# Block-product groups: one bank with four products, copied out on the way, in place of four banks with sums

## The chip, the cores and the metric

One core of a Trainium2 chip runs the whole program. The metric is the device time of one execution in microseconds. The core's engines work from queues of their own and meet at semaphores: TensorE (PE in the profile; PEld is its weight load), VectorE (DVE), ScalarE (ACT), GpSimd (POOL) and SyncE (SP), which issues most DMAs. TensorE writes into eight PSUM banks; each bank holds a tile of 128 x 448 fp32 here.

## The reference

The program computes an attention with mixed heads, then two gated or squared feed-forward layers, in fp32 accuracy:

```python
def _moe_ref(x, w1, w2, w3, w_out):
    a = x @ w1
    b = x @ w2
    h = a * b @ w3
    return (h @ w_out).astype(np.float32)

def _moe2_ref(x, w_in, w_out):
    h = np.maximum(x @ w_in, 0.0)
    return (h * h @ w_out).astype(np.float32)
```

x has 1792 tokens of 768 features (attention output); w1 and w2 go to 1024, w3 and w_out of the first layer are multiplied together ahead of use (their product is 1024 x 768), w_in goes to 2048 and the last w_out back to 768.

## The kernel before, in words

Each fp32 operand is split into a high part and a low part, and each product of a 128 x 128 weight block with 128 x 448 values takes three matmuls (high x high, high x low, low x high: `mm3`, L60). The tokens are done in two halves of 896, each in two tiles t = 0, 1 of 448.

Attention comes first. After it, `Moe.run` works through a list of units. A unit is a `l1` product (x by w1 or w2), `p34` (w3 by w_out), `ly` (a*b by that product, giving y), a "quad" or `l4_part` (h by the last w_out, in four groups of rows `gr`). The quads are what the change touches. A quad is a 2 x 2 block product (two 128-row output blocks r = 0, 1, two token tiles t = 0, 1) done with seven block products in place of eight. Its left factors are the weight blocks A(r, c) and four sums S1 to S4 of them, its right factors are B11, B21, B22 and four differences T1 to T4. With ks = 3 each product is 9 matmuls, so a quad is 63. There are 24 quads: 8 for x by w1 and w2 in the second half (`l1_quad`, j = 0 to 3, named q00, q01, q10, ... for w1 and w2 in turn) and 8 for y by w_in in each half (`l3_quad`, named qh00 to qh07 and qh10 to qh17). The hidden-layer quads come in runs between groups of `l4_part`: 0, 1, 2; 3, 4; 5, 6, 7 in the first half, and 0, 1, 2; 3, 4; 5, 6; 7 in the second. The last quad of each run (`hold`) lets its later work wait some steps longer.

A quad's result is finished by the other engines. In `quad.run`, the seven products t = 0 to 6 (this t is a step) go to four banks: A, B, C, A, B, C, D. ScalarE copies s1 (product 0) and s5 (product 2) out, VectorE forms u2 (product 1 plus s1) and u3 (bank B after its second product, plus s1), and `done(r, t, x, y)` takes each of the four results, as a bank alone (0, 0) or as a sum of two operands. `done` of a hidden-layer quad then applies relu and square, and `split_late` makes the high part on ScalarE (L723) and the low part on VectorE (L724). For (1, 1) the sum is on GpSimd, and relu and square on ScalarE (L877, L878); elsewhere they are one VectorE instruction (L881).

The order on every queue is the order in which the code issues, and nothing reorders it. `stage(s, run)` issues one step: loads, the sums S of weight blocks on VectorE (`combine`, L144) for products that are four or five steps ahead, the high part of a weight three steps ahead on ScalarE (`high`, L120), the low part two steps ahead on GpSimd (`rest`, L148), then whatever was put into `self.late[0]` for this step, then the matmuls of the product with the work that follows from it. `self.late[n]` holds work to be issued n steps after the next one's start.

Of the kernel before, what the change touches and what calls it, by code (L numbers as in the profile page):

```python
# [37 lines left out]
def fused_kernel(ctx, tc, q, k, v, w_pre, w_post, w1, w2, w3t, wo, win, wo2, eye, out):  # L38
# [494 lines left out]
    class Moe:  # L533
# [52 lines left out]
        def stage(self, s, run=None):  # L586
            w = self.w
            ok = lambda i: 0 <= i < len(self.pieces)
            quad = lambda i: self.pieces[i][1] if ok(i) and self.pieces[i][0] is None else None
            if ok(s + 6) and not quad(s + 6):  # L590
                w.load(s + 6, *self.pieces[s + 6][:2])
            if quad(s + 7) and self.pieces[s + 7][2] == ("A", 0, 0):
                w.load_quad(quad(s + 7))
            if quad(s + 5) and self.pieces[s + 5][2] == ("S", 2, 0):
                w.combine(quad(s + 5), 1)
                w.combine(quad(s + 5), 2)
            if quad(s + 4) and self.pieces[s + 4][2] in (("S", 3, 0), ("S", 4, 0)):
                w.combine(quad(s + 4), self.pieces[s + 4][2][1])
            if quad(s + 3):
                _, q, name = self.pieces[s + 3]  # L600
                w.ft[s + 3] = q.f[name]
                w.place(s + 3)
                w.high(s + 3)
            if ok(s + 4):
                w.narrow(s + 4)
            if ok(s + 3) and not quad(s + 3):
                for part in range(2):
                    w.join(s + 3, part)
                to = self.pieces[s + 3][2:]
                w.place(s + 3, self.wot[to[0]] if to and to[0] else None)  # L610
                if not self.pieces[s + 3][1]:
                    w.high(s + 3)
            if ok(s + 2):
                w.rest(s + 2, nc.vector if self.pieces[s + 2][2:] and not quad(s + 2) else nc.gpsimd)
            if run:
                self.late.append([])
                for f in self.late.pop(0):
                    f()
                run()
            if ok(s + 3) and not quad(s + 3) and self.pieces[s + 3][1]:  # L620
                w.high(s + 3)
                if s + 3 in self.keep:
                    w.save(s + 3, self.keep[s + 3])
# [172 lines left out]
        def quad(self, name, src, x, ks, done):  # L796
            q = type("Quad", (), {})()
            q.name, q.f, q.src = name, {}, src
            A, S_ = (lambda r, c: ("A", r, c)), (lambda n: ("S", n, 0))
            plan = [  # L800
                (A(0, 0), "B11", "A"), (S_(2), "T2", "B"), (S_(1), "T1", "C"), (A(0, 1), "B21", "A"),
                (S_(3), "T3", "B"), (S_(4), "B22", "C"), (A(1, 1), "T4", "D"),
            ]
            bank, tmp = {}, {}

            def us(n):
                tmp[n] = self.tile(f"{n}{name}")
                return tmp[n]

            def run(ws, t):  # L810
                _, xn, bk = plan[t]
                start = bk not in bank
                if start:
                    bank[bk] = self.psum(f"q{name}{bk}")
                acc = bank[bk]
                mm3(acc, [(self.chunk([ws[t]], c), x()[xn, c]) for c in range(ks)], start, True, not start)
                if t == 0:
                    nc.scalar.activation(us("s1"), acc, AF.Copy)
                elif t == 1:
                    self.add(us("u2"), acc, tmp["s1"])  # L820
                elif t == 2:
                    nc.scalar.activation(us("s5"), acc, AF.Copy)
                elif t == 3:
                    done(0, 0, acc)
                elif t == 4:
                    self.add(us("u3"), acc, tmp["s1"])
                    done(1, 1, tmp["u3"], tmp["s5"])
                elif t == 5:
                    done(0, 1, acc, tmp["u2"])
                else:  # L830
                    done(1, 0, acc, tmp["u3"])

            return [(None, q, n) for n, _, _ in plan], run

        def l1_quad(self, j, second):
            end = j == 3

            def done(r, t, x, y=None):
                m = 2 * j + r
                eng = nc.gpsimd if r and t and not end else nc.vector  # L840
                if not second:
                    a = self.xy["a", m, t] = self.tile(f"a1_{m}_{t}")
                    if y is None:
                        nc.scalar.activation(a, x, AF.Copy)
                    else:
                        self.add(a, x, y, eng)
                    return
                ab = self.xy["ab", 1, m, t] = self.pair(f"ab1_{m}_{t}")
                p = self.tile(f"p1_{m}_{t}")
                mul = lambda: nc.vector.tensor_tensor(p, x if y is None else p, self.xy["a", m, t], ALU.mult)  # L850
                if eng is nc.gpsimd:
                    self.late[0].append(lambda: self.add(p, x, y, eng))
                    self.late[1].append(mul)
                    self.split_late(ab, p, 2, 3)
                    return
                if y is not None:
                    self.add(p, x, y)
                mul()
                self.split_late(ab, p, 0, 0 if end else 1)

            src = [w12d[int(second), 2 * j + r] for r in range(2)]
            return self.quad(f"{j}{int(second)}", src, lambda: self.xq, 3, done)
# [1 line left out]
        def l3_quad(self, hf, j):  # L864
# [3 lines left out]
            def done(r, t, x, y=None):  # L868
# [3 lines left out]
                if y is None:  # L872
                    nc.scalar.activation(p, x, AF.Relu)
                    square = lambda: nc.scalar.activation(p, p, AF.Square)
                elif r and t and not end:
                    def square():
                        nc.scalar.activation(p, p, AF.Relu)  # L877
                        nc.scalar.activation(p, p, AF.Square)  # L878
                    self.late[0].append(lambda: self.add(p, x, y, nc.gpsimd))
                else:  # L880
                    square = lambda: nc.vector.scalar_tensor_tensor(p, p, 0.0, p, ALU.max, ALU.mult)  # L881
                    self.add(p, x, y)
                if end and y is not None:
                    square()
                    self.split_late(hb, p, 0, 0)
                    return
                at = {(0, 0): 0, (1, 1): 1, (0, 1): 0, (1, 0): 0}[r, t]
                if hold:
                    at = {(0, 0): 3, (1, 1): 2, (0, 1): 2, (1, 0): 1}[r, t]
                self.late[at].append(square)  # L890
                self.split_late(hb, p, at + 1, at + 2)

# [3 lines left out]
        def yquad(self, hf, n, t, acc):  # L896
# [28 lines left out]
            if name == "B22":  # L925
# [3 lines left out]
                hi("B22", acc)  # L929
                lo("T2", r("T2"))  # L930
                lo("B22", acc)
                diff("T4", r("B21"), r("T2"))
                hi("T3", r("T3"))
                hi("T4", r("T4"))
                lo("T3", r("T3"), G if j < 2 else V)
                lo("T4", r("T4"), G if j < 2 else V)
                return
            nc.scalar.activation(raw(name), acc, AF.Copy)
            if name != "B12":
# [50 lines left out]
        def l4_part(self, hf, gr, es):  # L990
            def run(ws, s):
# [2 lines left out]
                if hf == 0 and gr > 1:  # L994
                    self.quad_x(6 * gr - 12 + es[0])
                accs = {(e, t): self.psum(f"l4{hf}_{gr}_{e}_{t}") for e in es for t in range(2)}
                for cs, order in (((0, 1), (0, 1)), ((2,), (0, 1)), ((3,), (1, 0))):
                    for w, e in zip(ws, es):
                        for t in order:
                            terms = [(self.chunk([w], c), self.xy["h", hf, 4 * gr + c, t]) for c in cs]  # L1000
# [140 lines left out]
```

## Time and profile before

| what | value |
|---|---|
| time, median of 3 runs | 1284.42 us (1283.98 to 1284.72) |
| time of the profiled execution | 1285.8 us |
| its span, first to last instruction | 1284.0 us |
| PE busy | 1252.7 us (98%) |
| DVE / ACT / POOL busy | 901.2 / 750.3 / 609.2 us |
| granted TensorE clock | 1.0 |

Busy time of PE is not idle-free time: matmuls overlap, and a matmul of 0.36 us starts every 0.20 us in the rows below. The chain that ended last gives the time that counts; where it names PE for a stretch without a break, only PE's work sets the time there. The profiled execution is 1.8 us longer than its span, and 1.4 us above the median of the timed runs.

### The profile page before, as it was taken

How to read it: one execution, taken by the hardware profiler on the slowest of the kernel's cores; microseconds unless marked ns; L12 is line 12 of the kernel's file. 1: busy time of each engine (PE TensorE's matmuls, PEld its weight loads, DVE VectorE, ACT ScalarE, POOL GpSimd, SP SyncE). 2: the span in 40 equal slices, each digit the busy share in tenths (PEclk: the TensorE clock that was granted, in tenths of full speed). 3: DMA queues.
4: the chain of work that ended last, by engine and by line, in shares of the span. 5: the costliest groups of instructions: out<-in, count | busy, mean ns of one | idle time of the engine just before them, and what ended most of it. 6: DMA issues, size and time to landing. Idle time of an engine off the chain costs nothing.

```text
span 1284.0 us, 23281 instructions
## 1 busy us (share of the span) xinstructions
PE 1252.7 (98%) x8398; PEld 1081.6 (84%) x8398; DVE 901.2 (70%) x1569; ACT 750.3 (58%) x1645; POOL 609.2 (47%) x633
## 2 busy tenths in 40 slices
PE   7999999999998999999999999999999999999998
PEld 3677777776775788899999999999999999999998
DVE  4889889788877966766476968689777328443543
ACT  5988889888887655555445654454444336452520
POOL 4354255246322612333357655455877457552621
PEclk9999999999999999999999999999999999999999
DMA  6666466566555767789552545174311221212312
GB/s 215 171 182 201 128 197 215 139 173 191 172 158 168 218 177 221 239 275 310 177 187 69 177 139 171 58 254 148 132 62 54 67 66 41 83 42 59 90 33 87
DMA packets 107463, 190.80 MB, mean 149 GB/s; under 512 B 21845, under 2 KB 73045, under 8 KB 106837
## 3 DMA queue, kind: packets, MB, share of 16 engines
q1 hardware_dynamic: 86928, 166.69, 42.9%
q10 hardware_dynamic: 20421, 22.63, 5.0%
q8 instruction: 66, 1.08, 0.3%
q14 instruction: 48, 0.39, 0.1%
HBM read 117.72 MB, written 33.03 MB: 117 GB/s over the span
## 4 chain that ended last, share of the span: by engine, by line
PE 82%; DVE 5%; issue 4%; DMA 4%; POOL 2%; ACT 2%; SPq 0%; ACTq 0%; DVEq 0%; POOLq 0%
PE l L60 22%; PE y L60 9%; PE sp L321 8%; PE p L60 5%; PE pv L438 5%; PE tp L386 5%; PE sc L295 4%; DMA r<-s 3%; DVE pl L377 2%; POOL wl L148 1%; DVE nm L327 1%; DMA kraw<-k 1%; DVE p L400 1%; ACT ph L361 1%; ACT p L335 1%
## 5 line engine op out<-in xcount | busy, mean ns | idle before, releaser
L148 POOL TENSOR_TENSOR wl<-f,wh 128x512 fp32r<-128x512 f32 (+1 forms) x72 | 90.8, 1262 | 174.6 <-ACT wh L120 151.3
L321 PE MATMUL sp<-r,kpre 120*120 120x448 f32 x360 | 158.6, 559 | 12.8 <-ACT p L335 7.0
L335 ACT ACTIVATE p<-sp,nm 120x448 f32<-120x448 f32 x180 | 113.6, 642 | 49.1 <-DVE nm L327 48.8
L377 DVE SCALAR_TENSOR_TENSOR pl<-p,sm,ph 120x448 f16<-120x448 f32 (+3 forms) x270 | 139.4, 570 | 0.3 <-POOL ph L363 0.3
L327 DVE TENSOR_REDUCE nm<-sp 120x1 f32<-120x448 f32 x180 | 107.3, 618 | 41.0 <-PE sp L321 37.2
L350 POOL TENSOR_SCALAR sm<-sm 120x2 f32<-120x2 f32 (+3 forms) x94 | 25.1, 267 | 203.7 <-ACT p L335 202.5
L386 PEld LDWEIGHTS <-ph 120*128 120x128 f16 x1260 | 92.9, 98 | 30.9 <-issue 23.9
L361 ACT ACTIVATE ph<-p,sm 120x448 f16<-120x448 f32 (+1 forms) x180 | 107.7, 663 | 16.6 <-DVE sm L355 13.2
L148 POOL TENSOR_TENSOR wl<-Sh,wh 128x384 fp32r<-128x384 f32 x64 | 77.6, 1229 | 76.0 <-ACT wh L120 67.7
L386 PE MATMUL tp<-kwh,ph 120*128 120x120 f16 x630 | 106.1, 217 | 4.1 <-ACT p L398 1.9
L321 PEld LDWEIGHTS sp<-r,kpre 120*120 120x120 f32 x360 | 57.8, 182 | 57.9 <-issue 20.9
L386 PE MATMUL tp<-kwh,pl 120*128 120x120 f16 x630 | 105.1, 216 | 0.0
L386 PE MATMUL tp<-kwl,ph 120*128 120x120 f16 x630 | 105.1, 216 | 0.0
L295 PE MATMUL sc<-kt,qh 128*110 128x448 f32 (+1 forms) x192 | 97.5, 508 | 2.2 <-DVE kt L259 1.5
L306 ACT ACTIVATE s<-sc 110x448 f32<-110x448 f32 (+1 forms) x186 | 90.5, 559 | 5.6 <-PE sc L295 5.2
L438 PE MATMUL pv<-p,v 128*64 128x110 f32 (+1 forms) x1536 | 81.0, 262 | 0.6 <-ACT xs L448 0.6
L438 PEld LDWEIGHTS pv<-p,v 128*64 128x64 f32 x1536 | 74.1, 137 | 4.0 <-ACT xs L448 0.9
L104 DVE TENSOR_SCALAR f<-y 128x384 int32<-128x384 int32 (+1 forms) x88 | 65.8, 748 | 15.4 <-ACT y L93 10.8
L148 POOL TENSOR_TENSOR wl<-quadh,wh 128x384 fp32r<-128x384 f32 x48 | 56.2, 1174 | 40.3 <-ACT wh L120 37.5
L400 DVE TENSOR_SCALAR p<-tp,iv 128x360 f32<-128x360 f32 x135 | 74.2, 577 | 1.2 <-PE tp L386 1.2
L148 POOL TENSOR_TENSOR wl<-raw,wh 128x512 fp32r<-128x512 f32 x48 | 63.5, 1334 | 22.3 <-ACT wh L120 17.5
L295 PE MATMUL sc<-kt,ql 128*110 128x448 f32 (+1 forms) x192 | 70.3, 366 | 0.0
(1979 smaller groups left out, 3863.2 us busy)
## 6 DMA issues: line engine op xcount, KB each, us to landing
r<-s SPq DMA_DIRECT2D x172, 210.0 KB
raw<-w SPq DMA_DIRECT2D x32, 384.0 KB
sraw<-win SPq DMA_DIRECT2D x32, 384.0 KB
quadh<-wind SPq DMA_DIRECT2D x32, 384.0 KB
raw<-wo SPq DMA_DIRECT2D x24, 512.0 KB
kraw<-k SPq DMA_DIRECT2D x24, 448.0 KB
raw<-w3t SPq DMA_DIRECT2D x16, 512.0 KB
qraw<-q SPq DMA_DIRECT2D x35, 220.0 KB
```

The lines of the kernel that those rows point to most:

```text
L60: nc.tensor.matmul(acc, w, x, start=(first and i == 0 and j == 0), stop=(last and i == n - 1 and j == 2), skip_group_check=again,)
L148: eng.tensor_tensor(self.out[i][1], self.ft.pop(i), f32(self.out[i][0]), ALU.subtract)
L295: nc.tensor.matmul(sc[:ic], t[:, hh * ic : hh * ic + ic], self.kt[b, h // 2][:, h % 2], start=(i == 0), stop=(i == 1))
L306: nc.scalar.activation(self.st[n][:ic, h], self.sc.pop((n, h))[:ic], AF.Copy)
L321: nc.tensor.matmul(t[:kk], self.kpre[:kk, :kk], self.rt.pop(g)[:kk], start=True, stop=True)
L327: nc.vector.tensor_reduce(nm[:kk], self.sp[g][:kk], AX.X, ALU.max, negate=True)
L335: nc.scalar.activation(p[:kk], self.sp.pop(g)[:kk], AF.Exp, bias=self.nm.pop(g)[:kk], accum_out=self.sm[g // 2][:kk, g % 2 : g % 2 + 1],)
L361: nc.scalar.activation(h[:, to], p[:, fr], AF.Copy, scale=sm)
L377: nc.vector.scalar_tensor_tensor(l[:, to], p[:, fr], sm, h[:, to], ALU.mult, ALU.subtract)
L386: nc.tensor.matmul(t[:, j], p[:, at : at + 128], w, start=(i == 0), stop=(i == 2))
L400: nc.vector.tensor_scalar(d, t[:, main], self.iv, None, ALU.mult)
L438: nc.tensor.matmul(t[64 * e : 64 * e + 64, x, :w], self.v[b][:, j, g], self.p2[n][:, j * NH + g, :w], start=(j == 0), stop=(j == JC - 1),)
```

## The change

The seven products are taken in another order and go to three banks: X, Z, X, Z, X, Y, X. Bank X collects four products one upon the other. ScalarE copies it out after the first (s1), second (u2) and third (u3) of them, and takes the fourth as result (1, 0). Bank Z collects two (ScalarE copies s5 after the first), bank Y one. The sums s1 + ... that gave u2 and u3 on VectorE are gone, as is the sum of (1, 0); (0, 0) is now a sum, so each quad has two sums fewer. Of each quad's results, (0, 1) is ready at step 3, (1, 1) at 4, (0, 0) at 5 and (1, 0) at 6. In a hidden-layer quad relu and square of (1, 1) are now one VectorE instruction, in place of two on ScalarE; those of (1, 0) are two on ScalarE, and (0, 0) has VectorE's. In `yquad` the last differences and their splits are put off by a step or two, and `l4_part` takes tile t = 1 first.

```diff
--- before.py
+++ after.py
@@ -591,7 +591,7 @@
                 w.load(s + 6, *self.pieces[s + 6][:2])
             if quad(s + 7) and self.pieces[s + 7][2] == ("A", 0, 0):
                 w.load_quad(quad(s + 7))
-            if quad(s + 5) and self.pieces[s + 5][2] == ("S", 2, 0):
+            if quad(s + 5) and self.pieces[s + 5][2] == ("S", 1, 0):
                 w.combine(quad(s + 5), 1)
                 w.combine(quad(s + 5), 2)
             if quad(s + 4) and self.pieces[s + 4][2] in (("S", 3, 0), ("S", 4, 0)):
@@ -798,14 +798,14 @@
             q.name, q.f, q.src = name, {}, src
             A, S_ = (lambda r, c: ("A", r, c)), (lambda n: ("S", n, 0))
             plan = [
-                (A(0, 0), "B11", "A"), (S_(2), "T2", "B"), (S_(1), "T1", "C"), (A(0, 1), "B21", "A"),
-                (S_(3), "T3", "B"), (S_(4), "B22", "C"), (A(1, 1), "T4", "D"),
+                (A(0, 0), "B11", "X"), (S_(1), "T1", "Z"), (S_(2), "T2", "X"), (S_(4), "B22", "Z"),
+                (S_(3), "T3", "X"), (A(0, 1), "B21", "Y"), (A(1, 1), "T4", "X"),
             ]
             bank, tmp = {}, {}
 
-            def us(n):
+            def us(n, acc):
                 tmp[n] = self.tile(f"{n}{name}")
-                return tmp[n]
+                nc.scalar.activation(tmp[n], acc, AF.Copy)
 
             def run(ws, t):
                 _, xn, bk = plan[t]
@@ -814,21 +814,16 @@
                     bank[bk] = self.psum(f"q{name}{bk}")
                 acc = bank[bk]
                 mm3(acc, [(self.chunk([ws[t]], c), x()[xn, c]) for c in range(ks)], start, True, not start)
-                if t == 0:
-                    nc.scalar.activation(us("s1"), acc, AF.Copy)
-                elif t == 1:
-                    self.add(us("u2"), acc, tmp["s1"])
-                elif t == 2:
-                    nc.scalar.activation(us("s5"), acc, AF.Copy)
-                elif t == 3:
-                    done(0, 0, acc)
+                if t in (0, 1, 2, 4):
+                    us(("s1", "s5", "u2", "", "u3")[t], acc)
+                if t == 3:
+                    done(0, 1, acc, tmp["u2"])
                 elif t == 4:
-                    self.add(us("u3"), acc, tmp["s1"])
                     done(1, 1, tmp["u3"], tmp["s5"])
                 elif t == 5:
-                    done(0, 1, acc, tmp["u2"])
-                else:
-                    done(1, 0, acc, tmp["u3"])
+                    done(0, 0, acc, tmp["s1"])
+                elif t == 6:
+                    done(1, 0, acc)
 
             return [(None, q, n) for n, _, _ in plan], run
 
@@ -842,21 +837,23 @@
                     a = self.xy["a", m, t] = self.tile(f"a1_{m}_{t}")
                     if y is None:
                         nc.scalar.activation(a, x, AF.Copy)
+                    elif r:
+                        self.late[0].append(lambda: self.add(a, x, y, eng))
                     else:
-                        self.add(a, x, y, eng)
+                        self.add(a, x, y)
                     return
                 ab = self.xy["ab", 1, m, t] = self.pair(f"ab1_{m}_{t}")
                 p = self.tile(f"p1_{m}_{t}")
                 mul = lambda: nc.vector.tensor_tensor(p, x if y is None else p, self.xy["a", m, t], ALU.mult)
-                if eng is nc.gpsimd:
+                if r and t:
                     self.late[0].append(lambda: self.add(p, x, y, eng))
-                    self.late[1].append(mul)
-                    self.split_late(ab, p, 2, 3)
+                    self.late[0 if end else 1].append(mul)
+                    self.split_late(ab, p, *((1, 1) if end else (2, 3)))
                     return
                 if y is not None:
                     self.add(p, x, y)
                 mul()
-                self.split_late(ab, p, 0, 0 if end else 1)
+                self.split_late(ab, p, 0, 1 - (end and not t))
 
             src = [w12d[int(second), 2 * j + r] for r in range(2)]
             return self.quad(f"{j}{int(second)}", src, lambda: self.xq, 3, done)
@@ -872,21 +869,23 @@
                 if y is None:
                     nc.scalar.activation(p, x, AF.Relu)
                     square = lambda: nc.scalar.activation(p, p, AF.Square)
-                elif r and t and not end:
-                    def square():
-                        nc.scalar.activation(p, p, AF.Relu)
-                        nc.scalar.activation(p, p, AF.Square)
-                    self.late[0].append(lambda: self.add(p, x, y, nc.gpsimd))
                 else:
                     square = lambda: nc.vector.scalar_tensor_tensor(p, p, 0.0, p, ALU.max, ALU.mult)
+                if r and t:
+                    self.late[0].append(lambda: self.add(p, x, y, nc.vector if end else nc.gpsimd))
+                elif r == 0:
                     self.add(p, x, y)
-                if end and y is not None:
-                    square()
-                    self.split_late(hb, p, 0, 0)
+                if end:
+                    if r and t:
+                        self.late[0].append(square)
+                        self.split_late(hb, p, 1, 1)
+                    else:
+                        square()
+                        self.split_late(hb, p, 0, t)
                     return
-                at = {(0, 0): 0, (1, 1): 1, (0, 1): 0, (1, 0): 0}[r, t]
+                at = {(0, 1): 0, (1, 1): 1, (0, 0): 0, (1, 0): 0}[r, t]
                 if hold:
-                    at = {(0, 0): 3, (1, 1): 2, (0, 1): 2, (1, 0): 1}[r, t]
+                    at = {(0, 1): 3, (1, 1): 2, (0, 0): 2, (1, 0): 1}[r, t]
                 self.late[at].append(square)
                 self.split_late(hb, p, at + 1, at + 2)
 
@@ -929,11 +928,15 @@
                 hi("B22", acc)
                 lo("T2", r("T2"))
                 lo("B22", acc)
-                diff("T4", r("B21"), r("T2"))
-                hi("T3", r("T3"))
-                hi("T4", r("T4"))
-                lo("T3", r("T3"), G if j < 2 else V)
-                lo("T4", r("T4"), G if j < 2 else V)
+
+                def rest():
+                    hi("T3", r("T3"))
+                    diff("T4", r("B21"), r("T2"))
+                    hi("T4", r("T4"))
+                    lo("T3", r("T3"), G if j < 2 else V)
+                    lo("T4", r("T4"), G if j < 2 else V)
+
+                self.late[1].append(rest)
                 return
             nc.scalar.activation(raw(name), acc, AF.Copy)
             if name != "B12":
@@ -994,7 +997,7 @@
                 if hf == 0 and gr > 1:
                     self.quad_x(6 * gr - 12 + es[0])
                 accs = {(e, t): self.psum(f"l4{hf}_{gr}_{e}_{t}") for e in es for t in range(2)}
-                for cs, order in (((0, 1), (0, 1)), ((2,), (0, 1)), ((3,), (1, 0))):
+                for cs, order in (((0, 1), (1, 0)), ((2,), (1, 0)), ((3,), (1, 0))):
                     for w, e in zip(ws, es):
                         for t in order:
                             terms = [(self.chunk([w], c), self.xy["h", hf, 4 * gr + c, t]) for c in cs]
```

Where the order of the queues matters is the hand-over from one hidden-layer quad to the next. The names: Sh01n is a sum S of quad 1's weight blocks, wh84 to wh87 are high parts of its weights, h20_f_t is the hidden value of row block f and tile t, h0_f_th its high and h0_f_tl its low part.

ScalarE, from the weights of quad 1 to its first copy s1, before:

```order
L120 ACTIVATE wh84_9634<-Sh012_9596 128x384 [waits DVE_49]
L723 ACTIVATE h0_0_0h_9611<-h20_0_0_9613 128x448 [waits Activation_49]
L120 ACTIVATE wh85_9653<-Sh011_9594 128x384 [waits Pool_49]
L877 ACTIVATE h20_1_1_9633<-h20_1_1_9633 128x448 [waits Pool_49]
L878 ACTIVATE h20_1_1_9633<-h20_1_1_9633 128x448 [waits Activation_49]
L120 ACTIVATE wh86_9681<-quadh010_9538 128x384
L723 ACTIVATE h0_1_1h_9631<-h20_1_1_9633 128x448 [waits Activation_49]
L723 ACTIVATE h0_0_1h_9649<-h20_0_1_9651 128x448 [waits DVE_49]
L818 ACTIVATE s1h01_9698<-qh01A_9688 128x448 [waits PE_49]
L120 ACTIVATE wh87_9702<-Sh013_9679 128x384 [waits DVE_49]
L723 ACTIVATE h0_1_0h_9671<-h20_1_0_9673 128x448 [waits DVE_49]
```

ScalarE there, now:

```order
L120 ACTIVATE wh84_9633<-Sh011_9593 128x384 [waits DVE_49,Pool_49]
L723 ACTIVATE h0_0_1h_9610<-h20_0_1_9612 128x448 [waits DVE_49]
L120 ACTIVATE wh85_9655<-Sh012_9595 128x384 [waits Pool_49]
L870 ACTIVATE h20_1_0_9673<-qh00X_9544 128x448 [waits PE_49]
L120 ACTIVATE wh86_9681<-Sh014_9653 128x384 [waits DVE_49]
L723 ACTIVATE h0_1_1h_9630<-h20_1_1_9632 128x448 [waits DVE_49]
L723 ACTIVATE h0_0_0h_9649<-h20_0_0_9651 128x448 [waits DVE_49]
L871 ACTIVATE h20_1_0_9673<-h20_1_0_9673 128x448 [waits Activation_49]
L808 ACTIVATE s1h01_9698<-qh01X_9688 128x448 [waits PE_49]
L120 ACTIVATE wh87_9700<-Sh013_9679 128x384 [waits DVE_49,Pool_49]
L723 ACTIVATE h0_1_0h_9671<-h20_1_0_9673 128x448 [waits Activation_49]
```

Ahead of s1 there now stand the high parts of (1, 1) and (0, 0) and the square of (1, 0); s1 had the high parts of (1, 1) and (0, 1) ahead of it before.

VectorE at the same place, from the sum at step 5 of quad 0 on, before:

```order
L794 TENSOR_TENSOR h20_0_1_9651<-qh00C_9582,u2h00_9576 128x448 [waits DMAHW0_49,PE_49]
L724 TENSOR_TENSOR h0_0_0l_9612<-h20_0_0_9613,h0_0_0h_9611 128x448 [waits Activation_49]
L881 SCALAR_TENSOR_TENSOR h20_0_1_9651<-h20_0_1_9651 128x448 [waits DVE_49]
L794 TENSOR_TENSOR h20_1_0_9673<-qh00D_9661,u3h00_9629 128x448 [waits PE_49]
L144 TENSOR_TENSOR Sh013_9679<-quadh010_9538,quadh011_9540 128x384 [waits Pool_49]
L881 SCALAR_TENSOR_TENSOR h20_1_0_9673<-h20_1_0_9673 128x448 [waits DVE_49]
L144 TENSOR_TENSOR Sh014_9700<-quadh010_9538,Sh012_9596 128x384 [waits Pool_49]
L724 TENSOR_TENSOR h0_1_1l_9632<-h20_1_1_9633,h0_1_1h_9631 128x448 [waits Activation_49]
```

VectorE there, now:

```order
L794 TENSOR_TENSOR h20_0_0_9651<-qh00Y_9639,s1h00_9554 128x448 [waits PE_49]
L144 TENSOR_TENSOR Sh014_9653<-quadh010_9534,Sh012_9595 128x384 [waits Pool_49]
L724 TENSOR_TENSOR h0_0_1l_9611<-h20_0_1_9612,h0_0_1h_9610 128x448 [waits Activation_49]
L873 SCALAR_TENSOR_TENSOR h20_1_1_9632<-h20_1_1_9632 128x448 [waits Pool_49]
L873 SCALAR_TENSOR_TENSOR h20_0_0_9651<-h20_0_0_9651 128x448 [waits DVE_49]
L144 TENSOR_TENSOR Sh013_9679<-quadh010_9534,quadh011_9536 128x384
L724 TENSOR_TENSOR h0_1_1l_9631<-h20_1_1_9632,h0_1_1h_9630 128x448 [waits Activation_49]
L724 TENSOR_TENSOR h0_0_0l_9650<-h20_0_0_9651,h0_0_0h_9649 128x448 [waits Activation_49]
```

Between the sum of step 5 and its relu-and-square there was one low part; now there are S4 (Sh014), a low part and the relu-and-square of (1, 1).

TensorE at the start of quad 1's third product (step 2), before, with the semaphores that it waits on:

```order
L60 MATMUL qh01B_9709<-y0T22l_9056,wh84_9634 128x448
L60 MATMUL qh01B_9709<-y0T22h_9055,wl84_9635 128x448
L60 MATMUL qh01C_9726<-y0_1h1_9041,wh85_9653 128x448 [waits Activation_49]
L60 MATMUL qh01C_9726<-y0_1l1_9042,wh85_9653 128x448
L60 MATMUL qh01C_9726<-y0_1h1_9041,wl85_9654 128x448 [waits Pool_49]
L60 MATMUL qh01C_9726<-y0_1h1_9041,wh85_9653 128x448
```

TensorE there, now:

```order
L60 MATMUL qh01Z_9707<-y0_1l1_9042,wh84_9633 128x448
L60 MATMUL qh01Z_9707<-y0_1h1_9041,wl84_9634 128x448
L60 MATMUL qh01X_9688<-y0T20h_9043,wh85_9655 128x448 [waits Activation_49]
L60 MATMUL qh01X_9688<-y0T20l_9044,wh85_9655 128x448
L60 MATMUL qh01X_9688<-y0T20h_9043,wl85_9656 128x448 [waits Pool_49]
L60 MATMUL qh01X_9688<-y0T21h_9049,wh85_9655 128x448
```

The third product goes into bank X, which s1 is copied from; it went into a bank of its own before.

## Rows read from the trace of the kernel before

**Rows 1.** The page: busy time by engine; granted TensorE clock in tenths.
```profile
PE 1252.7 (98%) x8398; PEld 1081.6 (84%) x8398; DVE 901.2 (70%) x1569; ACT 750.3 (58%) x1645; POOL 609.2 (47%) x633
...
PEclk9999999999999999999999999999999999999999
```

**Rows 2.** What PE waited for: from whom, us in all, times, longest us.
```profile
PE sp L321 <- ACT p L335: 7.0, 10, 1.6
...
PE p L60 <- POOL wl L148: 1.6, 2, 0.9
...
PE l L60 <- POOL wl L148: 0.4, 1, 0.4
```

**Rows 3.** Chain that ended last: start us, us, what.
```profile
716.26 1.80 PE qh02B L60 x9
...
955.68 1.80 PE q20A L60 x9
```

**Rows 4.** Program's end: start us, us, engine, line, operation.
```profile
1279.35 0.37 PE L60 MATMUL l<-h_0h,wl 128*128 128x448 f32 x1
1279.75 1.16 DVE L794 TENSOR_TENSOR o<-l,oa 128x448 f32<-128x448 f32 x2 [3.65 <-PE l L60]
```

**Rows 5.** Stretches with quads: us, busy us (count) of PE, PEld, DVE, ACT, POOL; clock.
```profile
690.00:727.00 37.00, 37.00 (x186) 34.48 (x186) 35.09 (x43) 24.36 (x50) 27.44 (x22) 1.00 0.27 83
...
905.00:1006.00 101.00, 101.00 (x507) 94.66 (x506) 70.63 (x94) 42.92 (x89) 72.76 (x64) 1.00 0.24 80
```

**Rows 6.** PE at the hand-over from quad 1 to quad 2 of hidden layer, first half.
```profile
716.10 0.36 PE L60 MATMUL qh02B<-y0T20h,wh 128*128 128x448 f32 x1
...
717.90 0.36 PE L60 MATMUL qh02C<-y_1h,wh 128*128 128x448 f32 x1
```

**Rows 7.** ScalarE (ACT) at the same hand-over, with idle time before.
```profile
715.35 1.03 ACT L723 ACTIVATE h_1h<-h 128x448 fp32r<-128x448 f32 x2
716.30 0.55 ACT L818 ACTIVATE s1h<-qh02A 128x448 f32<-128x448 f32 x1
...
718.34 0.58 ACT L723 ACTIVATE h_0h<-h 128x448 fp32r<-128x448 f32 x1 [0.84 <-DVE h L881]
```

**Rows 8.** VectorE (DVE) at the same hand-over.
```profile
712.70 0.63 DVE L794 TENSOR_TENSOR h<-qh01C,u2h 128x448 f32<-128x448 f32 x1
713.24 1.04 DVE L724 TENSOR_TENSOR h_0l<-h,h_0h 128x448 fp32r<-128x448 f32 x1
714.21 1.45 DVE L881 SCALAR_TENSOR_TENSOR h<-h 128x448 f32<-128x448 f32 x1
...
716.87 1.44 DVE L881 SCALAR_TENSOR_TENSOR h<-h 128x448 f32<-128x448 f32 x1
```

**Rows 9.** GpSimd (POOL) there.
```profile
712.65 1.16 POOL L794 TENSOR_TENSOR h<-u3h,s5h 128x448 f32<-128x448 f32 x1 [1.03 <-ACT wh L120]
713.76 2.77 POOL L148 TENSOR_TENSOR wl<-Sh,wh 128x384 fp32r<-128x384 f32 x2
```

**Rows 10.** The squares on DVE in all hidden-layer quads: ns min/median/max.
```profile
L881 DVE SCALAR_TENSOR_TENSOR h<-h x16: 612/1026/1445, 701.6 to 856.8; 128x448 f32<-128x448 f32 x16
```

**Rows 11.** DVE between quads 5 and 6.
```profile
822.16 1.44 DVE L881 SCALAR_TENSOR_TENSOR h<-h 128x448 f32<-128x448 f32 x1
...
824.05 0.84 DVE L144 TENSOR_TENSOR Sh<-quadh,quadh 128x384 f32<-128x384 f32 x1
824.82 0.61 DVE L881 SCALAR_TENSOR_TENSOR h<-h 128x448 f32<-128x448 f32 x1
```

**Rows 12.** POOL between quads 5 and 6.
```profile
823.08 1.39 POOL L148 TENSOR_TENSOR wl<-quadh,wh 128x384 fp32r<-128x384 f32 x1
825.53 1.24 POOL L148 TENSOR_TENSOR wl<-Sh,wh 128x384 fp32r<-128x384 f32 x1 [1.06 <-ACT wh L120]
```

**Rows 13.** A hand-over of the first layers' quads: ACT.
```profile
958.50 0.58 ACT L723 ACTIVATE ab_0h<-p 128x448 fp32r<-128x448 f32 x1 [0.78 <-DVE p L850]
958.99 0.53 ACT L818 ACTIVATE s<-q20A 128x448 f32<-128x448 f32 x1
```

## The prediction

> **What bounds the kernel now.** Start with the page. PE is busy for 1252.7 of 1284.0 us and its clock is granted in full in all slices [rows 1]. That alone doesn't say that PE has no idle time, so the next view is what PE waited for: its long waits are in the attention (L321 at the head), and on the line of the feed-forward matmuls, L60, they come to 1.6 us in `p34` and a few tenths in units named l; no quad is in that list [rows 2]. The chain of waits says the same in order of time: each product of a quad follows the one before after 1.80 us, which is 9 matmuls at 0.20 us, through the hidden-layer quads and through those of w1 and w2 [rows 3]. So TensorE sets the time wherever the change acts, and nothing waits behind it to be won: 24 quads of 63 matmuls stay 24 quads of 63 matmuls, at the same pace. What the change can do is make TensorE wait. In the hidden-layer quads the helpers have little room: VectorE is busy for 35.09 of 37.00 us, ScalarE for 24.36, GpSimd for 27.44; in the quads of w1 and w2 there is more, 70.63 and 42.92 of 101.00 us on the first two [rows 5]. The program's end, from the last matmul at 1279.35 us over two sums to the last DMA [rows 4], is not touched.
>
> **The change part by part.** Counts come from the order of the queues: VectorE has 33 instructions fewer, ScalarE 18 more, and PE, GpSimd and SyncE as many as before.
>
> Sums removed: two per quad. A sum that reads a bank takes VectorE 0.54 us from its start to the next one's (712.70 to 713.24) [rows 8]. In the quads of w1 and w2 that is 1.1 us of VectorE per quad. In a hidden-layer quad one relu-and-square comes to VectorE instead (0.61 to 1.45 us [rows 10]), so its work there stays about what it was. No part of this lies on TensorE's path: worth nothing.
>
> Copies added: u2 and u3, 0.55 us each as s1 takes now [rows 7]; in hidden-layer quads ScalarE loses relu and square of (1, 1) for them. In the other eight quads 16 copies, 8.8 us, go beside 101 us in which ScalarE works 42.92 [rows 5]: nothing, as long as no copy is late for bank X.
>
> Bank X returning after one product is the part that counts. A copy starts 0.20 us after the last matmul of its product was issued plus that matmul's 0.20: s1 at 716.30 when the next product's first matmul was issued at 716.10 [rows 6, 7]. It takes 0.55 us, and the next product into X wants to start 1.80 us after 716.10. So a punctual copy leaves 1.80 - 0.20 - 0.55 = 1.05 us. For u2 and u3 ScalarE has at most two weight parts queued ahead: hidden, with that cover. For s1 it is not so at a hand-over from one hidden-layer quad to the next. Ahead of s1, ScalarE now has the high part of (0, 0), which waits for VectorE's relu-and-square of (0, 0), and the square of (1, 0). Before, it had the high part of (0, 1) there, whose square ended at 714.21 + 1.45 = 715.66; two high parts from 715.35 on ended just ahead of s1 at 716.30 [rows 7, 8]. Nobody waited for s1 for three products then.
>
> I count from the issue of the quad's first matmul, 716.10 - 1.80 = 714.30. VectorE's sum of step 5 starts at -1.60 (712.70) and leaves VectorE free at -1.06. Then it has four instructions with both operands in SBUF, where there were two: S4, a low part, the square of (1, 1), the square of (0, 0). What each costs depends on GpSimd. The same square took 1.44 us at 822.16 and 0.61 at 824.82; GpSimd was inside instructions until 823.08 + 1.39 = 824.47 and then idle until 825.53 [rows 11, 12]. So one GpSimd instruction in the way costs 0.83 us. With none, the four take 0.48 + 0.54 + 0.55 + 0.61, and end at 1.12 (the first is an estimate, the 0.55 of such a sum less the 0.07 by which pitch is under duration). After that: 0.03 to ScalarE (716.87 + 1.44 = 718.31, ScalarE at 718.34 [rows 7, 8]), a high part 0.48 (half of 716.30 - 715.35), the square at the same price, s1 0.55, and 0.03 back: 1.57. The third product wants to start at 3.60, so the squares must be done by 2.03: one GpSimd instruction in the way is just free, two cost 0.75 us, three 1.58, four 2.41.
>
> How many are in the way? GpSimd's sum of (1, 1) waited for VectorE's u3 and started at 712.65, which is -1.65 [rows 9]. It now waits for ScalarE's copy u3, which ends at -3.60 + 0.20 + 0.55 = -2.85, so it ends by -1.7 (1.11 us from its start to the next). Three weight low parts follow at about 1.0 us when free: from -1.7, from -0.7, and the third once its high part wh86 is made, which is behind the relu of (1, 0) at 0.20: at about 1.2. S4 starts at -1.06 inside the first and loses 0.29 (the 0.84 row, pitch 0.77 [rows 11]); the low part starts at -0.3 inside the second and takes 1.40; the square of (1, 1) gets through at 0.55 ahead of the third; the square of (0, 0) starts at 1.65 inside the third and takes 1.45. Sum: -1.06 + 0.77 + 1.40 + 0.55 + 1.45 = 3.11; with 1.57 it is 4.68 against 3.60. TensorE waits 1.1 us. The bounds of this term are 0 and 2.41. I take 1.1, which lies between two and three collisions.
>
> A rule bears on this. SBUF — State Buffer of the Trainium skill, section Who interferes with whom, says that a VectorE instruction with two SBUF inputs and a GpSimd instruction that reads SBUF lock a common port pair for a whole instruction, the one that starts first; the trace agrees (0.61 against 1.44 us). By that rule the count above holds, 1.1 us; priced by medians without it (the low part's 0.97 and the squares' 1.03 [rows 8, 10], S4 0.77) the squares end at -1.06 + 0.77 + 0.97 + 0.96 + 1.03 = 2.67 and the wait is 0.64.
>
> Hand-overs of this kind: 0-1, 1-2, 3-4, 5-6, 6-7 in the first half, 0-1, 1-2, 3-4, 5-6 in the second, nine. Quads that follow other units find nothing late, and a quad that holds its work is followed by `l4_part`. 9 x 1.1 = 9.9 us.
>
> From a w2 quad to the next w1 quad there are three hand-overs. s1 of q20 ran from 958.99 to 959.52, behind the high part of (1, 0) [rows 13]; q20's first matmul was issued 0.16 ahead of the chain's 955.68, at 955.52 [rows 3, 6], and X would be wanted at 959.12. With the order as it was that is 0.4 us late; now (1, 0) is multiplied straight from its bank, one sum earlier, but behind S4. Bounds 0 and 0.9 (one collision more), value 0.1 as the two edits about cancel: 0.3 us.
>
> Other edits cost nothing. `yquad` puts T3 and T4 off, but T2 is now wanted at product 2 in place of 1, 1.8 us more. `l4_part` takes t = 1 first, and the t = 1 results are now the earlier ones. S4 a step earlier is counted above.
>
> Sum: 9.9 + 0.3 = 10.2 us. The profiled execution would go from 1285.8 to 1296.0, its span from 1284.0 to 1294.2. The timed median lies 1.4 below the profiled execution: 1284.4 + 10.2 = 1294.6 us.
>
> **The rivals.** *No wait at all, hence no change.* If at most one GpSimd instruction lies in VectorE's way, the squares are done by 2.03 and s1 is in time. For it: a VectorE that enters the hand-over with less queued, and GpSimd runs 1.1 us earlier, so its low parts may be over sooner. Against it: the third low part cannot start before wh86 at 1.2, just where the last square comes. Time: 1284.4, with up to 0.25 us per hand-over 1286.7.
>
> *VectorE late on entry.* At 35.09 of 37.00 us [rows 5] it may start the sum of step 5 late, with all four instructions blocked: 9 x 2.41 + 3 x 0.9 = 24.4 us, 1308.8. Against it: the wait itself gives VectorE time to catch up. Perfetto Trace Analysis of the Trainium skill, section Matmuls, advises that independent groups rotate through different PSUM banks so that evacuation overlaps the next group; products 0 and 2 share one here. Rows 7 show 1.05 us of cover for a punctual copy, so by the trace the rule costs only where the copy is late.
>
> *Faster.* It would need TensorE waits in quads to remove, and there are none [rows 2, 3].
>
> **How the numbers follow.** A measurement of this kernel tells 0.2%, 2.6 us, from no change. Waits of 0.3 to 1.8 us at the nine hand-overs: 0.74. No wait: 0.16. VectorE late: 0.08. Faster for a reason not seen: 0.02. That is 0.82 slower, 0.16 within, 0.02 faster. The range from 1285 to 1302 leaves out most of the second case below and the third above.
>
> **What would show it.** PE waits on ScalarE's s1 at the third product of quads 1, 2, 4, 6, 7 and 11, 12, 14, 16, about 1.1 us each, and at no other place; s1 starting some 4.1 us after its quad's first matmul, behind a high part that waits for VectorE's square. Right in kind and wrong in size if these waits are 0.3 or 2 us. Wrong if PE's third products follow after 1.80 us, or if the waits sit at u2, u3 or in the quads of w1 and w2.

## The result, and the profile after

The changed kernel takes 1298.62 us, median of 4 runs (1297.29 to 1301.27), against 1284.2 us for the kernel before (4 runs). The ratio is 1.0114, 95% interval 1.0097 to 1.0132: slower, by more than was forecast (1294.6), inside the range. The profiled execution took 1297.86 us with a span of 1296.1, 12.1 us more than the profiled execution of the kernel before in both. Timed again beside the kernel before, the ratio was 1.0091 (the last experiment).

The page of the changed kernel, busy time by engine and the granted clock:

```profile
PE 1256.0 (97%) x8398; PEld 1081.1 (83%) x8398; DVE 870.1 (67%) x1536; ACT 753.4 (58%) x1663; POOL 605.0 (47%) x633
...
PEclk9999999999999999999999999999999999999999
```

VectorE works 31 us less than in [rows 1], ScalarE 3 us more, PE's clock is at its higher level, 2.4 GHz, in the row of slices as before, and the span is longer all the same. Busy time doesn't tell why. The list of PE's waits does, in which no quad stood before [rows 2] (from whom, us in all, times, longest):

```profile
PE qh01X L60 <- ACT s1h L808: 0.9, 1, 0.9
...
PE qh16X L60 <- ACT s1h L808: 0.8, 1, 0.8
...
PE qh10Z L60 <- ACT s5h L808: 0.3, 1, 0.3
PE qh00Z L60 <- ACT s5h L808: 0.3, 1, 0.3
```

Nine such rows name s1, each at the third product of a hidden-layer quad: 01, 02, 04, 06, 07 and 11, 12, 14, 16. Two more name s5 at the first quad of each half. The hand-over from quad 1 to quad 2, which [rows 6 to 9] show for the kernel before, reads as follows. TensorE (start us, us, engine, line, operation):

```profile
719.63 0.37 PE L60 MATMUL qh02Z<-y_1h,wl 128*128 128x448 f32 x1
720.81 0.47 PE L60 MATMUL qh02X<-y0T20h,wh 128*128 128x448 f32 x1 [0.81 <-ACT s1h L808]
721.12 0.36 PE L60 MATMUL qh02X<-y0T20l,wh 128*128 128x448 f32 x1
```

The third product starts 1.18 us after the matmul before it, in place of 0.20, and its first matmul keeps PE 0.31 us, in place of 0.20. So the hand-over costs 1.09 us, while the list says 0.8: it counts from the modelled end of the matmul before. A loss on a pipelined engine is read from start to start.

ScalarE at the same place:

```profile
717.92 0.58 ACT L723 ACTIVATE h_1h<-h 128x448 fp32r<-128x448 f32 x1 [0.54 <-DVE h L873]
719.28 0.58 ACT L723 ACTIVATE h_0h<-h 128x448 fp32r<-128x448 f32 x1 [0.78 <-DVE h L873]
719.77 0.56 ACT L871 ACTIVATE h<-h 128x448 f32<-128x448 f32 x1
720.23 0.52 ACT L808 ACTIVATE s1h<-qh02X 128x448 f32<-128x448 f32 x1
```

In [rows 6 and 7] s1 started 2.0 us after the quad's first matmul, 0.20 after the first matmul of the next product. That first matmul is now at 716.23 (719.63 + 0.20 - 3.60), and s1 starts 4.00 us after it, behind a high part that had waited for VectorE, and a square. VectorE:

```profile
714.63 0.62 DVE L794 TENSOR_TENSOR h<-qh01Y,s1h 128x448 f32<-128x448 f32 x1 [1.56 <-PE qh01Y L60]
715.17 0.83 DVE L144 TENSOR_TENSOR Sh<-quadh,Sh 128x384 f32<-128x384 f32 x1
715.92 1.44 DVE L724 TENSOR_TENSOR h_1l<-h,h_1h 128x448 fp32r<-128x448 f32 x1
717.28 1.97 DVE L873 SCALAR_TENSOR_TENSOR h<-h 128x448 f32<-128x448 f32 x2
```

The sum of step 5 at 714.63 is 1.60 us ahead of the quad's first matmul, as in [rows 8]. Then come S4, the low part that takes 1.44 us, and the two squares, 1.97 us together, the second of them done at 719.25. GpSimd:

```profile
713.45 1.16 POOL L794 TENSOR_TENSOR h<-u3h,s5h 128x448 f32<-128x448 f32 x1 [0.87 <-ACT u3h L808]
714.57 2.30 POOL L148 TENSOR_TENSOR wl<-Sh,wh 128x384 fp32r<-128x384 f32 x2
717.46 1.30 POOL L148 TENSOR_TENSOR wl<-Sh,wh 128x384 fp32r<-128x384 f32 x1 [0.59 <-ACT wh L120]
```

Its sum starts at 713.45, 2.78 us ahead (it was 1.65 in [rows 9]), two low parts of weights follow back to back, and the third starts at 717.46, 1.23 us after the first matmul. These are the three instructions that VectorE met. The other eight hand-overs have the same rows: the sum of step 5 starts 1.60 us ahead of the quad's first matmul, the squares are done 3.02 to 3.10 us after it, and s1 starts at 4.00 to 4.09.

A step is the time from one matmul's start to the next one's; what it takes above 0.20 us is called loss here. All steps over 0.23 us, from the first quad to the last matmul, sum to 11.9 us of loss; in the kernel before they sum to 0.1 us.

| where | loss, us |
|---|---|
| third product of nine hidden-layer quads, late start | 8.9 |
| the first matmul after each of these waits, 0.31 in place of 0.20 | 1.0 |
| fourth product of quads 00 and 10 (s5), start and first matmul | 1.2 |
| third product of q10, q20, q30, start and first matmul | 0.6 |
| q00, a low part of a weight | 0.1 |

The small steps are not in the waits' list. This is q10's third product:

```profile
940.16 0.36 PE L60 MATMUL q10Z<-x1h,wl 128*128 128x448 f32 x1
940.48 0.47 PE L60 MATMUL q10X<-T20h,wh 128*128 128x448 f32 x1
940.79 0.36 PE L60 MATMUL q10X<-T20l,wh 128*128 128x448 f32 x1
```

It starts 0.32 us after its predecessor, then 0.31: 0.23 us lost in which PE, by its modelled ends, was never idle.

### The profile page after: what moved, and what is told of

The parts are those of the page before. It is cut to its first block, busy times and chain, and to the rows that moved or that the text cites. A ratio compares the mean times of both kernels' runs of the same rounds, so it can differ in the third digit from the quotient of the medians.

```text
span 1296.1 us, 23238 instructions
## 1 busy us (share of the span) xinstructions
PE 1256.0 (97%) x8398; PEld 1081.1 (83%) x8398; DVE 870.1 (67%) x1536; ACT 753.4 (58%) x1663; POOL 605.0 (47%) x633
## 4 chain that ended last, share of the span: by engine, by line
PE 77%; DVE 9%; issue 4%; DMA 4%; ACT 3%; POOL 2%; SPq 0%; ACTq 0%; DVEq 0%; POOLq 0%
PE l L60 22%; PE y L60 9%; PE sp L321 8%; PE tp L386 5%; PE p L60 5%; PE pv L438 5%; PE sc L295 4%; DMA r<-s 2%; DVE pl L377 2%; DVE h L873 1%; POOL wl L148 1%; DVE nm L327 1%; DVE h_1l L724 1%; DMA kraw<-k 1%; DVE p L400 1%
## 5 line engine op out<-in xcount | busy, mean ns | idle before, releaser
L148 POOL TENSOR_TENSOR wl<-Sh,wh 128x384 fp32r<-128x384 f32 x64 | 73.1, 1152 | 105.6 <-ACT wh L120 105.6
L148 POOL TENSOR_TENSOR wl<-raw,wh 128x512 fp32r<-128x512 f32 x48 | 66.5, 1399 | 17.9 <-ACT wh L120 13.5
L104 DVE TENSOR_SCALAR f<-y 128x384 int32<-128x384 int32 (+1 forms) x88 | 60.0, 682 | 21.9 <-ACT y L93 11.6
L60 PE MATMUL l<-h_0h,wl 128*128 128x448 f32 x192 | 69.7, 363 | 0.0
```

The lines of the kernel that those rows point to most:

```text
L60: nc.tensor.matmul(acc, w, x, start=(first and i == 0 and j == 0), stop=(last and i == n - 1 and j == 2), skip_group_check=again,)
L148: eng.tensor_tensor(self.out[i][1], self.ft.pop(i), f32(self.out[i][0]), ALU.subtract)
```

## The experiments

Three theories stood against each other. The first is that of the prediction: s1 is late by the order of ScalarE's queue, behind VectorE's instructions that meet GpSimd's. The second: a bank that is wanted again after one product is simply too soon. The third: the added copies are too much work for ScalarE. The kernels of the first four runs were timed together; the kernel before took 1286.2 us there, median of 33 runs (1284.42 to 1289.09), some 2 us more than in the first comparison. So times are compared as ratios ("more than before" is the ratio, in us), and the losses in the quads come from the traces: the same sum of long steps as above, 11.9 us for the changed kernel.

**s1 ahead of the late work.** `ahead` is true at step 0 of every quad.

```diff
...
                 self.late.append([])
-                for f in self.late.pop(0):
+                late = self.late.pop(0)
+                if ahead:
+                    run()
+                for f in late:
                     f()
-                run()
+                if not ahead:
+                    run()
...
+                ahead = it and self.units[it[0]][0][0][0] is None and it[1] < 1
...
```

> ScalarE's copy s1 is issued ahead of the late work of the quad before, in all quads; nothing else moves. Late copy by queue order: the nine waits on s1 of 0.8 to 0.9 us in the trace (each delays its product by 1.06 us and its first matmul more, some 1.2 us) go, and so do the 0.2 us at the three w2-to-w1 hand-overs. Left are two waits on s5 behind T3 and T4 (0.3 in the record) and s5 behind the two high parts, which is now due at about 5.5 us against 5.4 wanted: 1284.2 + 1.2 + 9 x 0.1 to 0.3 = 1286 to 1288. Bank rival (a bank that returns after one product makes TensorE wait, whatever the queues): no gain, 1298. ScalarE-load rival (too many copies): no gain, 1298.

Measured: 1289.64 us, ratio 1.0022 (1.0013 to 1.0031), 2.8 us more than before; loss in the quads 3.1 us. ScalarE at the hand-over from quad 1 to 2:

```profile
717.55 0.55 ACT L813 ACTIVATE s1h<-qh02X 128x448 f32<-128x448 f32 x1 [0.84 <-PE qh02X L60]
717.99 0.57 ACT L728 ACTIVATE h_1h<-h 128x448 fp32r<-128x448 f32 x1
...
720.44 0.52 ACT L813 ACTIVATE s5h<-qh02Z 128x448 f32<-128x448 f32 x1
```

s1 starts at 717.55 as soon as its product is through (0.84 us idle ahead of it, for PE). Every wait on s1 is gone, in the quads of w1 and w2 too. The late work now lies ahead of s5, which ends at 720.96, and PE shows that:

```profile
720.75 0.36 PE L60 MATMUL qh02X<-y0T22h,wl 128*128 128x448 f32 x1
721.02 0.47 PE L60 MATMUL qh02Z<-y_1h,wh 128*128 128x448 f32 x1
721.33 0.36 PE L60 MATMUL qh02Z<-y_1l,wh 128*128 128x448 f32 x1
```

The fourth product starts 0.27 us after its predecessor, and its first matmul takes 0.31: 0.18 us here, 0.17 to 0.19 at seven more of the nine and 0.24 at quad 01, besides the 1.2 us at quads 00 and 10 of the hidden layer and 0.2 at q00. With the same banks and the same copies 8.7 of 11.9 us are gone, so the second and the third theory fall.

**s1 and s5 ahead of it.** The same edit for steps 0 and 1 (`it[1] < 2`).

> s1 and s5 are both issued ahead of the late work. Late copy by queue order: no wait of TensorE on any copy is left in any quad, so the time is that of the kernel before, 1284.2 to 1285; the 48 sums fewer are worth nothing, as TensorE sets the time. If the sums are worth something, under 1283. Bank rival and ScalarE-load rival: 1298.

Measured: 1287.16 us, ratio 1.0004 (0.9995 to 1.0013): no difference from the kernel before. Loss in the quads 0.8 us, and no quad in the list of waits. The chain of waits at the same hand-over (start us, us, what):

```profile
718.38 1.80 PE qh02Z L60 x9
720.18 1.81 PE qh02X L60 x9
721.99 1.86 PE qh02Z L60 x9
```

Products follow at 1.80 us, with 0.06 us lost once. The expectation of no wait at all was not quite met: the late work of step 0 still lies between s1 and s5, and the fourth product of quads 01 and 11 waits for s5 (0.29 and 0.25 us), those of 02 and 12 lose 0.05 each, and q00 loses 0.17 at a low part of a weight. This is the best form of the change: three banks and 48 sums fewer, and it doesn't beat the four banks. As TensorE lost only 0.1 us there in the kernel before, there was nothing for the sums to give back.

**Square of (1, 1) back on ScalarE.**

```diff
...
+                elif r and t and not end:
+                    def square():
+                        nc.scalar.activation(p, p, AF.Relu)
+                        nc.scalar.activation(p, p, AF.Square)
                 else:
                     square = lambda: nc.vector.scalar_tensor_tensor(p, p, 0.0, p, ALU.max, ALU.mult)
...
```

> Relu and square of (1, 1) go back to two ScalarE instructions, as in the kernel before; VectorE loses one instruction of the four at a hand-over, ScalarE gains one per quad. Collision count: the squares are then done by -1.06 + 0.77 + 1.40 + 0.55 = 1.66 us after the quad's first matmul, under the 2.03 that s1 needs, so the nine waits go; left are the waits on s5 and the three w2-to-w1 hand-overs: about 1286.5. ScalarE-load rival: 15 quads with more work on ScalarE, waits longer than now, over 1299. Bank rival: 1298.

Measured: 1288.43 us, ratio 1.0016 (1.0006 to 1.0026), 2.1 us more than before; loss in the quads 2.1 us. ScalarE has 30 instructions more than in the changed kernel, and the nine waits are gone. VectorE at the hand-over:

```profile
714.26 0.62 DVE L794 TENSOR_TENSOR h<-qh01Y,s1h 128x448 f32<-128x448 f32 x1 [1.51 <-PE qh01Y L60]
714.80 0.83 DVE L144 TENSOR_TENSOR Sh<-quadh,Sh 128x384 f32<-128x384 f32 x1
715.55 1.44 DVE L724 TENSOR_TENSOR h_1l<-h,h_1h 128x448 fp32r<-128x448 f32 x1
716.91 0.61 DVE L877 SCALAR_TENSOR_TENSOR h<-h 128x448 f32<-128x448 f32 x1
```

Three instructions stand behind the sum in place of four, and the square is done at 717.52; it was 719.25. ScalarE:

```profile
717.56 0.58 ACT L723 ACTIVATE h_0h<-h 128x448 fp32r<-128x448 f32 x1
718.04 0.56 ACT L871 ACTIVATE h<-h 128x448 f32<-128x448 f32 x1
718.51 0.52 ACT L808 ACTIVATE s1h<-qh02X 128x448 f32<-128x448 f32 x1
```

s1 ends at 719.03. The quad's first matmul is at 715.86 here (VectorE's sum less 1.60 us ahead, as above), the third product is wanted at 719.46, and it gets its bank in time. The square is done 1.66 us after that first matmul, as worked out in the expectation (1.66 to 1.73 at all nine). One VectorE instruction decides over 9.9 us, and more work on ScalarE does no harm: this strikes the third theory again.

**GpSimd only writes.** In the hidden-layer quads:

```diff
...
-                w.rest(s + 2, nc.vector if self.pieces[s + 2][2:] and not quad(s + 2) else nc.gpsimd)
+                if quad(s + 2) and quad(s + 2).name[0] == "h" and s + 2 in w.ft:
+                    nc.gpsimd.memset(f32(w.out[s + 2][1]), 0.0)
+                    w.ft.pop(s + 2)
+                else:
+                    w.rest(s + 2, nc.vector if self.pieces[s + 2][2:] and not quad(s + 2) else nc.gpsimd)
...
```

> In the hidden-layer quads GpSimd fills the low parts of the weights with zeros instead of subtracting (that part of the product is left out), so GpSimd reads SBUF there for its one sum per quad only. If a GpSimd instruction that reads is what makes VectorE's two-operand instructions take 1.4 in place of 0.6 us: the four end at about 1.1 to 1.5, the nine waits go, 1286 to 1287. If these instructions are slow for another reason (TensorE's or ScalarE's reads, or the queue alone), the waits stay: 1297 to 1299.

Measured: 1286.94 us, ratio 1.0006 (0.9997 to 1.0016): no difference from the kernel before; loss in the quads 0.8 us. VectorE at the hand-over:

```profile
712.42 0.62 DVE L798 TENSOR_TENSOR h<-qh01Y,s1h 128x448 f32<-128x448 f32 x1 [2.25 <-PE qh01Y L60]
712.96 0.55 DVE L144 TENSOR_TENSOR Sh<-quadh,Sh 128x384 f32<-128x384 f32 x1
713.42 0.62 DVE L728 TENSOR_TENSOR h_1l<-h,h_1h 128x448 fp32r<-128x448 f32 x1
713.96 1.15 DVE L877 SCALAR_TENSOR_TENSOR h<-h 128x448 f32<-128x448 f32 x2
```

And GpSimd:

```profile
712.34 2.23 POOL L615 MEMSET wl<- 128x384 f32 x6
```

All four instructions run at their short durations, 0.55, 0.62 and 1.15 us for the two squares, though GpSimd is at work beside them from 712.34 to 714.57, writing zeros. So it is not GpSimd being busy that makes them long, but its subtractions, which read SBUF. The fills wait for no high part and so come in bunches, at other moments than the subtractions; that they don't slow VectorE rests on this overlap, which the trace has at all nine hand-overs. A fill also takes less time than a subtraction (2.23 us for six, against 2.30 for two), and no run has GpSimd read for as short a time. What is left of the loss lies in the quads of w1 and w2, where GpSimd subtracts as before.

**The changed kernel again.**

> The changed kernel as it is, timed beside the kernel before on one chip in as many rounds as the second experiment. In the two profiled executions the changed kernel's span is 12.1 us longer, and the stretched steps between matmuls in the quads sum to 11.9 us; the few timed runs so far differ by 14.4 us. If the steps in the quads are all of it: 11 to 13 us more than before. If something that the trace of one execution does not show comes on top (a lower clock after waits, for one): 14 us or more, with the clock of the profiled run under that of before.

Measured: 1297.58 us, median of 4 runs (1296.86 to 1298.44), before 1285.66 us, median of 7 (1284.14 to 1288.14); ratio 1.0091 (1.0074 to 1.0108), and the medians are 11.9 us apart. Loss in the quads 11.9 us in this execution too. The steps in the quads are all of it, within the interval, and no lower clock comes on top: the mean granted clock is 0.998 over these runs of either kernel. The traces say the same. From the first quad's first matmul to the last matmul the two profiled executions of the changed kernel take 602.12 and 602.14 us, that of the kernel before 590.34, and without the loss 590.2 to 590.3 us are left in each of the seven traces. The stretch ahead of it, up to the first quad, takes 688.6 to 690.9 us in them, without order by kernel. The 14.4 us of the first comparison are 2.5 us more than the steps explain, about as much as that earlier stretch varies; its interval of 1.0097 to 1.0132 overlaps this one. What made it larger is not settled, as only one of its executions of the changed kernel was traced.

## Why the prediction was right

- **The place.** The nine hand-overs named are the nine rows of the waits, and no other third product of a hidden-layer quad waits. The order of s1 behind a high part that waits for VectorE is in ScalarE's rows. The sign "at no other place" did not hold: some 2 us of the loss lie in quads 00 and 10 of the hidden layer and in those of w1 and w2.
- **The count of collisions.** Worked out: S4 frees VectorE after 0.77 us, the low part after 1.40, the squares are done at 3.11. Measured: 0.75, 1.36 and 3.02. The two squares did come as one short, one long (1.97 together). GpSimd's three starts were -1.7, -0.7 and 1.2 by the count; its low parts came at -1.66, -0.69 and 1.23. The fourth run shows that the collisions are the cause, the third that one of them fewer is enough. Priced by medians and not by collisions, the forecast was 0.64 us a hand-over, under every late start measured.
- **The size per hand-over.** 1.1 us forecast, 9.9 us for nine; 9.9 us measured. The two parts of it were not foreseen as such: a start about 1.0 us late (0.98 to 1.06), and 0.11 us because the first matmul after a wait is slower. The count put the squares' end 0.09 us too late, and this made up for the part left out: that the sum came out to the tenth is luck, the mechanism is not.
- **The quads of w1 and w2.** 0.3 us forecast for the three, 0.6 measured, half of it the slower first matmul, which the prediction put at nothing.
- **What was missed: the first quad of each half.** The step that failed is "Quads that follow other units find nothing late", with "Other edits cost nothing" on `yquad`. The high parts of T3 and T4, put off to step 1, stand ahead of s5 there:

```profile
693.19 0.53 ACT L120 ACTIVATE wh<-Sh 128x384 fp32r<-128x384 f32 x1 [1.16 <-DVE Sh L144]
693.63 0.56 ACT L917 ACTIVATE y0T32h<-y0T3raw 128x448 fp32r<-128x448 f32 x1
694.09 0.56 ACT L917 ACTIVATE y0T42h<-y0T4raw 128x448 fp32r<-128x448 f32 x1
694.56 0.52 ACT L808 ACTIVATE s5h<-qh00Z 128x448 f32<-128x448 f32 x1
```

They come after a weight's high part that waits until 693.19 for VectorE's S3, so s5 starts at 694.56 and the fourth product, due at 694.66, waits until 695.13. In the second run s5 stands ahead of them and these two losses, 1.2 us, are gone. The order is half of the cause: S3 came late by a collision of the same kind. S3 on VectorE and the low part on GpSimd in the changed kernel, then S3 in the fourth run:

```profile
691.68 1.01 POOL L148 TENSOR_TENSOR wl<-Sh,wh 128x384 fp32r<-128x384 f32 x1 [2.68 <-ACT wh L120]
691.80 1.30 DVE L144 TENSOR_TENSOR Sh<-quadh,quadh 128x384 f32<-128x384 f32 x1
```

```profile
691.36 0.55 DVE L144 TENSOR_TENSOR Sh<-quadh,quadh 128x384 f32<-128x384 f32 x1
```

In the fourth run, with the order as in the changed kernel, S3 takes 0.55 us in place of 1.30 and both losses are gone too.
- **The sum.** 10.2 us forecast, 11.9 found in the trace: 1.2 us from the first quads, 0.3 from those of w1 and w2, 0.1 in q00, nothing from the hand-overs. The first timed difference is larger than either.
- **The rivals.** No wait at all: wrong as it stood, but it is what the second (nearly) and the fourth run bring about at the nine hand-overs. There products 0 and 2 share a bank as before, so the shared bank costs only where the copy is late, as was argued from [rows 7]. VectorE late on entry: no, it was idle for 1.56 us ahead of the sum of step 5, and for 1.06 to 1.91 us at the nine. Faster: nothing to gain, shown by the second run.

## What to carry to other kernels

Before work is taken off a helper engine, read whether the bounding engine ever waits for it; here it lost 0.1 us in all from the first quad on, so 48 sums fewer could not show. When an accumulation is read out on the way and then continued, the copy becomes a deadline for TensorE: count what stands ahead of it in its in-order queue, and what those instructions wait for, and issue the copy ahead of everything that can be late. An instruction's duration belongs to its neighbours as much as to itself: price VectorE's two-operand instructions by what GpSimd reads at that moment, not by their mean.

## What the runs showed of the hardware that was not expected

After each of the 15 waits in the quads of the changed kernel, and of the 12 in the first experiment, the first matmul kept TensorE 0.31 to 0.32 us until the next one started, in place of 0.20, whether the matmul was 0.04 us late or 1.06 us. Each such stop costs 0.11 us more than its wait, and many short stops cost more than a list of waits says, or don't appear there at all.

The rows of the weight load (PEld) go with this. In the changed kernel, for the last matmul ahead of the wait at quad 2 that is shown above and for the first behind it:

```profile
719.43 0.19 PEld L60 LDWEIGHTS qh02Z<-y_1h,wl 128*128 128x128 f32 x1
720.81 0.19 PEld L60 LDWEIGHTS qh02X<-y0T20h,wh 128*128 128x128 f32 x1 [1.19 <-ACT s1h L808]
```

The load for the matmul at 719.63 starts at 719.43, 0.20 us ahead of it. The load behind the wait starts at 720.81 together with its matmul, and the next matmul, at 721.12, follows 0.31 us after that load. Two steps of 0.25 us in the second experiment and one of 0.28 us in the kernel before are smaller cases of the same; this is one of them, in the second experiment:

```profile
721.77 0.19 PEld L60 LDWEIGHTS qh02Z<-y_1h,wh 128*128 128x128 f32 x1 [0.16 <-ACT s5h L813]
721.83 0.41 PE L60 MATMUL qh02Z<-y_1h,wh 128*128 128x448 f32 x1
722.08 0.37 PE L60 MATMUL qh02Z<-y_1l,wh 128*128 128x448 f32 x1
```

The load starts only 0.06 us ahead of its matmul, and the next matmul again follows 0.31 us after the load, so the step is 0.25 us. In all seven traces there are 58 places in the quads where a load starts less than 0.06 us ahead of its matmul, and in each the next matmul starts 0.31 to 0.32 us after that load. So the added 0.11 us fits a weight load that a wait leaves uncovered; no run tests this by itself.

The granted clock did not fall for stops of about a microsecond: its row on the page is as before, and its mean over the runs of the last experiment is 0.998 for both kernels.
